# Output tiles of three query blocks: feed-forward and attention part added in one PSUM bank, with the gate ratio moved into the softmax reciprocals

## The chip, the cores and the metric

The kernel runs on one core of a Trainium2 chip. The core has five engines that run side by side and meet only at semaphores: TensorE (PE, matrix products), VectorE (DVE), ScalarE (ACT), GpSimd (POOL, used here to issue DMAs) and SyncE (SP, which issues the other DMAs). Matrix products land in PSUM, which has eight banks of 128 partitions x 512 fp32. The metric is the device time of one execution in microseconds; the number before is the median of three runs.

## The reference

One input x (2048 rows of 512 numbers) goes through two branches whose results are mixed by a gate, a number per row.

```python
g = sigmoid((x * gate_w).sum(-1, keepdims=True))
a = softmax(q @ k^T / 4) @ v, for 32 heads of 16 numbers, then @ wo      # q, k, v = x @ wqkv
b = (silu(x @ w_gate) * (x @ w_up)) @ w_down                             # 1792 columns inside
out = g * a + (1 - g) * b
```

Nearly all of the work on elements is the softmax: 32 heads x 2048 queries x 2048 keys, 134 million exponentials.

## The kernel before, in words

**Units and tiles.** The 2048 queries are cut into four blocks of 512 (`QB`, numbers 0 to 3), the heads into eight groups of four (`G`). A unit is one block with one group; there are 32 (`UNIT`). The first group of all four blocks comes first, then blocks 0, 1, 2, 3 with their other seven groups each. A unit has 16 slots, one for each 128 keys (`KT`); a slot is one tile: four heads x 128 keys x 512 queries of scores, so there are 512 tiles in all.

**Two ways to the exponential.** Most tiles go to ScalarE: `emit_pair` makes two heads' scores in one double bank `s_t` (two of them take turns), and one ACTIVATE of 128x1024 writes the exponentials `e_t`. A tile takes two of these. The rest goes to VectorE: `emit_d` makes one head's scores in a bank `d_t`, VectorE evicts it to 16-bit integers (`y_t<-d_t`, four times for a tile), and then corrects the whole 128x2048 tile: a mask (`z_t<-y_t`), an affine step (`u_t`, `kaug` or `wd_t` `<-z_t`), a square, a product, an addition, and a last step (`y_t<-y_t`). The addition is made by an accumulating DMA from GpSimd (line 795), or, in the last unit and if the end is near, on VectorE (`add_here`). Buffers named u_t, kaug and wd_t are places for the same intermediate.

**Value products.** `pv` multiplies a tile of exponentials with the values into one bank `o_ps`, which after 16 tiles holds a unit's outputs, and, in every 32nd row, the softmax denominators. `post` copies it to `osb`. `settle` sends the rows of `osb` by DMA to `onc[qb]` (the block's attention outputs) and the denominators to DRAM (`dd`). When a block has all its groups, `recip` reads the denominators back as 128x128 (`dn`), waits until its slot, takes reciprocals (`rn`), stores them (`rr`), spreads them by DMA over the partitions (`rb`) and multiplies `onc` by them (`norm`). For block 3 it does so for the first six groups; the last two are normalised separately at the end.

**Feed-forward.** For a block, 14 chunks of 128 hidden columns each need a gate and an up product (`gu`), a tanh on ScalarE (`th<-gu`), and two VectorE steps that leave the hidden activations in `mt`. Then for each 128 queries `down_pieces` accumulates 14 steps of `w_down` in a bank `dps`; VectorE evicts it to `bblk`, scaled by 1 - g (`omg`) for blocks 0 to 2, or by exp(-logit) (`ge`) for block 3. `fin_pieces` accumulates four steps of `wo` in a bank `a_ps`; `store` evicts it as g * a_ps + bblk (`gval` is g) and sends it out. For block 3 the sum of both parts is made in PSUM at the end (`last_pieces`, `tail`): `bblk` enters through a product with the identity, and the final eviction multiplies by g, since g * exp(-logit) = 1 - g.

**What sets the order.** The program is one unrolled list for each engine; `ordered` (helper lines 158, 161 and 170 of the profile) keeps each engine's instructions in the order in which they were written. A planner written in the kernel decides that order, with assumed costs: `plan.pe`, `plan.dve` and `plan.act` are the times to which each engine is booked. Score pairs for ScalarE come first; what fits between two pairs is value products, VectorE scores or a piece of a side chain. `Pacer` holds the side chains, each with a release slot, a due slot and a condition; the chain due first is taken. `later` hands VectorE an eviction, `fill_dve` picks VectorE's next work. Three banks (`ps_m`) serve `d_t` and all side chains.

`v_unit` decides how many tiles VectorE takes: it gives a tile from the end of a unit when VectorE, by the plan, would be done with it `LEAD` (16 us) before ScalarE gets to the end of that unit, or `LAST` (11 us before the change) for the last unit. So a shorter list of VectorE work becomes more VectorE tiles and fewer ScalarE exponentials by itself.

Of the kernel before, what the change touches and what calls it, by code (L numbers as in the profile page):

```python
# [9 lines left out]
ALU = mybir.AluOpType  # L10
AX = mybir.AxisListType
BF16 = mybir.dt.bfloat16
F32 = mybir.dt.float32
# [66 lines left out]
def kernel(  # L80
# [13 lines left out]
    P = 128  # L94
    x = A_x.flatten_outer_dims()
    S, D = x.shape
    F = B_w_gate.shape[1]
    DH = 16
    H = D // DH
    G = H // 4  # L100
    NB = H // 8
    DC = D // P
    FC = F // P
    KT = S // P
    QBW = 512
    QB = S // QBW
    TQ = QBW // P
    assert H * DH == D and D % P == 0 and F % P == 0 and S % QBW == 0 and G == 8 and TQ == 4
    out_f = out.flatten_outer_dims()
# [3 lines left out]
    SLOTS = UNITS * KT  # L113

    UNIT = [(qb, 0) for qb in range(QB)] + [(qb, g) for qb in range(QB) for g in range(1, G)]
# [165 lines left out]
    gval = const.tile([P, KT], F32, name="gval")  # L281
    omg = const.tile([P, KT], F32, name="omg")
    ge = const.tile([P, KT], F32, name="ge")
    bblk = big.tile([P, TQ, D], BF16, name="bblk")


# [20 lines left out]
    def later(cost, f, ready=None, key=None):  # L307

        c = plan.chain
        if c is not None:  # L310
            c.owed += 1
        ready = plan.pe + 0.25 if ready is None else ready
        owed.insert(sum(o[0] <= ready for o in owed), (ready, cost, f, c, key))
# [101 lines left out]
    def columns(n, name, lhs, rhs, end, c0=0):  # L415

        st = {}

        def pc(k):
            def f():  # L420
                if k == 0:
                    st["p"] = m_tile(name)
                w, r = lhs(k), rhs(k)
                for j in range(4):
                    mm(st["p"][32 * j:32 * j + 32, c0:QBW], lhsT=w[:, 32 * j:32 * j + 32], rhs=r, start=(k == 0),
                       stop=(k == n - 1), tile_position=(0, 32 * j), skip_group_check=True)
                spend("C", 1)
                if k == n - 1:
                    end(st["p"])
            return f  # L430
        return [(1, pc(k), k == 0) for k in range(n)]
# [180 lines left out]
    def gate_pieces(t0):  # L612
        def f():
            gp = m_tile("glog")
            for t in (t0, t0 + 1):
                for dc in range(DC):
                    mm(gp[:, t:t + 1], lhsT=xT[:, dc, t * P:(t + 1) * P],
                       rhs=gw_col[:, dc:dc + 1], start=(dc == 0), stop=(dc == DC - 1))
            spend("F", 2)

            def end():
                vec.tensor_scalar(out=ge[:, t0:t0 + 2], in0=gp[:, t0:t0 + 2], scalar1=-60.0, scalar2=60.0,
                                  op0=ALU.max, op1=ALU.min)
                m_free(gp, plan.dve)
            later(0.15, end)
        return [(0.7, f, True, "F", None)]

    def gate_end():
        act(out=ge[:, :], in_=ge[:, :], func=ACT.Exp, scale=-1.0)
        plan.act += 0.2  # L630

        def end():
            vec.tensor_scalar(out=omg[:, :], in0=ge[:, :], scalar1=1.0, scalar2=None, op0=ALU.add)
            vec.reciprocal(gval[:, :], omg[:, :])
            vec.tensor_tensor(out=omg[:, :], in0=ge[:, :], in1=gval[:, :], op=ALU.mult)
        later(0.5, end, plan.act + 0.2)


    FS = [(qb, fc) for qb in range(QB) for fc in range(FC)]
    w_gate, w_up, gs_of = {}, {}, {}  # L640

    def w_load(i, gate):
# [31 lines left out]
    scaled = set()  # L674

    def down_pieces(qb, tq):

        def end(p):
            t, n = tq, qb * TQ + tq
            share = omg if qb < QB - 1 else ge  # L680
            vec.tensor_scalar(out=bblk[:, t, :], in0=p[:, 0:D], scalar1=share[:, n:n + 1],
                              scalar2=None, op0=ALU.mult)
            if qb == QB - 1:
                scaled.add(t)
            m_free(p, plan.dve)
        return columns(FC, "dps", lambda fc: mt[:, fc, tq * P:(tq + 1) * P], lambda fc: wd_t[:, fc, :],
                       lambda p: later(0.65, lambda: end(p)))
# [238 lines left out]
    def recip16(o, i):  # L926
        with nc.allow_low_precision(reason="bf16 reciprocal of softmax denominators is plenty accurate here"):
            vec.reciprocal(o, i)

    def recip(qb, g1, n0):  # L930

        n = 4 * g1
        dn = work.tile([P, P], BF16, tag="dn", name="dn")
        queue.dma_start(out=dn[0:4 * n, :], in_=dds[qb][0:n, :].rearrange("h (a c) -> (h a) c", c=P))

        def spread():
            rn = work.tile([P, P], BF16, tag="rn", name="rn")
            recip16(rn[0:4 * n, :], dn[0:4 * n, :])
            rr = dram.tile([H, QBW], BF16, tag="rr", name="rr")
            queue.dma_start(out=rr[0:n, :].rearrange("h (a c) -> (h a) c", c=P), in_=rn[0:4 * n, :])  # L940
            for b in range(g1 // 2):
                queue.dma_start(out=rb[:, b, :],
                                  in_=rr[8 * b:8 * b + 8, :].unsqueeze(1).broadcast_to([8, DH, QBW]))
        at.setdefault(n0 + 6, []).append(lambda: later(0.87, spread))
        for b in range(g1 // 2):
            def norm(b=b):
                vec.tensor_tensor(out=onc[qb][:, b, :], in0=onc[qb][:, b, :], in1=rb[:, b, :], op=ALU.mult)
                normed.add((qb, b))
            at.setdefault(n0 + 13 + b, []).append(lambda norm=norm: later(0.345, norm))

    def recip_here(osb):
# [2 lines left out]
        mm(dps[:, :], lhsT=sbc_t[:, :], rhs=osb[:, :], start=True, stop=True)  # L954
        rd = work.tile([P, QBW], BF16, tag="rd", name="rd")
        return dps, rd

    def store(t, a_ps, base, o_t=None):
        if o_t is None:
            o_t = opool.tile([P, D], BF16, tag="ot", name="o_t")[:, :]  # L960
        vec.scalar_tensor_tensor(out=o_t, in0=a_ps[:, 0:D], scalar=gval[:, t:t + 1], in1=base,
                                 op0=ALU.mult, op1=ALU.add)
        queue.dma_start(out=out_f[t * P:(t + 1) * P, :], in_=o_t)

    here_done = []
    a_ps = []
# [6 lines left out]
    def last_pieces():  # L973

        def keep(pa, pb):
            a_ps.extend([pa, pb])
        return two_banks(NB + 1, "a_l", last_rows(0), last_rows(1), keep, stop=False)
# [16 lines left out]
            w, r = last_rows(tq)(i)  # L994
            mm(a_ps[tq][:, 0:D], lhsT=w, rhs=r, start=(i == 0), stop=False)

    def fin_pieces(qb, tq):

        def end(p):
            store(qb * TQ + tq, p, bblk[:, tq, :])  # L1000
            m_free(p, plan.dve)
        return columns(NB, "a_ps", lambda b: onc[qb][:, b, tq * P:(tq + 1) * P], lambda b: wo_t[:, b, :],
                       lambda p: later(0.67, lambda: end(p)))

    kp0 = ps_s.tile([P, 2 * QBW], F32, tag="s", name="kp0")
    qp0 = m_tile("qp0")
# [164 lines left out]
    gates = [pace.add([(0.2, gate_end, False)], 40, 106, gates)]  # L1171

    prev = []
    fin_prev = []
    ffn = set()
    f0, f1 = 72, SLOTS - 8
    per = (f1 - f0) / QB
    for qb in range(QB):
        a0 = f0 + per * qb
        gus = []  # L1180
        for i in range(FC * qb, FC * qb + FC):
            gate_pcs, up_pcs = gu_chain(i)

            def first(f=gate_pcs[0][1], i=i):
                if i == 0:
                    w_load(0, True)
                    w_load(0, False)
                    w_load(1, True)
                    w_load(1, False)
                w_load(i + 2, True)  # L1190
                w_load(i + 2, False)
                f()
            for k, pcs in enumerate(([(1, first, True)] + gate_pcs[1:], up_pcs)):
                prev = [pace.add(pcs, 58, a0 + per * (0.6 if qb < QB - 1 else 0.68) * (i + 0.5 + k / 2 - FC * qb) / FC, begun=prev)]
                gus += prev
                ffn.update(prev)
        for tq in range(TQ):
            c = pace.add(down_pieces(qb, tq), 0 if qb else 100, a0 + per * (0.6 + 0.3 * (tq + 1) / TQ if qb < QB - 1 else 0.68 + 0.32 * (tq + 1) / TQ), (gus if tq == 0 else prev) + fin_prev + gates)
            prev = [c]
            ffn.add(c)  # L1200
        last = qb == QB - 1
        fin_prev = []
        if last:

            def ripe():
                return (all((qb, b) in normed for b in range(NB - 1)) and len(scaled) == TQ and here_done)
            pace.add(last_pieces(), SLOTS - KT // 2, SLOTS, prev, cond=ripe)
            break
        for tq in range(TQ):
            rel = (UNIT.index((qb, G - 1)) + 1) * KT + 24  # L1210
            dl = max(a0 + per * (0.9 + 0.1 * (tq + 1) / TQ), rel + 7 + 3 * tq)

            def cond(qb=qb):
                return all((qb, b) in normed for b in range(NB))
            fin_prev.append(pace.add(fin_pieces(qb, tq), rel, dl, prev + fin_prev, cond=cond))


    au = at_ = half = 0
# [134 lines left out]
        emit_pv(ns[0])  # L1353

    SLACK = 0.1
    LEAD, LAST = 16.0, 11.0
    TILE_US = 1.87

    def forward():
# [183 lines left out]
```

## Time and profile before

The median is 829.81 us (829.46 to 830.11). The profiled execution spans 827.6 us.

| engine | busy, us | share | main work |
|---|---|---|---|
| ScalarE | 810.9 | 98% | 844 exponentials of 128x1024, 787.6 us |
| VectorE | 794.8 | 96% | 90 tiles of exponentials; evictions |
| TensorE | 784.2 | 95% | 8115 matmuls |
| GpSimd | 102.2 | 12% | 90 accumulating DMAs |

How to read it: a group's line gives the engine, the operation, what it writes and reads, the number of instructions, then the busy time, the mean duration of one record in ns, and the engine's idle time just before them with what ended it. Records of neighbouring instructions on one engine overlap, so the duration of a record is longer than the distance to the next one. A line of waits reads "who waited <- for whom: us in total, times, longest". A line of the timeline reads start, length, engine, operation, and in brackets the idle time before it.

### The profile page before, as it was taken

The page shows a single profiled execution, that of the slowest core. Times are in us where ns is not written, and L with a number is a line of the kernel's source. Part 1 is how long each engine was busy: PE and PEld are TensorE (multiplying, and loading weights), DVE is VectorE, ACT ScalarE, POOL GpSimd, SP SyncE. Part 2 cuts the span into 40 slices and gives each one's busy share as a digit, 9 for nine tenths or more (in the row PEclk, how much of TensorE's full clock was granted, in tenths as well). Part 3 has the DMA queues.
Part 4 walks back from the last instruction along what each step waited for, and adds up shares of the span by engine and source line. Part 5 has one row for each costly group of instructions (what it writes and reads, how often), then busy time and mean ns, then how long its engine had stood idle before and what let it go on. Part 6 is the DMA issues. An engine that isn't in the chain of part 4 may idle for free. (4 is left out here: it accounts for less than half of the span.)

```text
span 827.6 us, 20391 instructions
## 1 busy us (share of the span) xinstructions
PE 784.2 (95%) x8115; PEld 232.7 (28%) x8116; DVE 794.8 (96%) x1175; ACT 810.9 (98%) x913; POOL 102.2 (12%) x124
## 2 busy tenths in 40 slices
PE   8999999999999999999999999999998999999996
PEld 3322332322222222222222222222222222222222
DVE  6899999999999999999999999999999999999994
ACT  6999999999999999999999999999999999999996
POOL 5010111100011101101110100101111101111100
PEclk9999999999999999999999999999999999999999
DMA  7034346675544445654435474544434455453333
GB/s 178 13 76 90 59 86 124 129 154 103 105 90 84 98 85 117 118 119 84 88 68 100 81 157 85 119 91 87 79 74 100 92 113 109 103 101 73 74 63 77
DMA packets 100615, 79.54 MB, mean 96 GB/s; under 512 B 75664, under 2 KB 88552, under 8 KB 100520
## 3 DMA queue, kind: packets, MB, share of 16 engines
q0 software_dynamic: 12960, 47.19, 30.8%
q1 hardware_dynamic: 85704, 30.60, 15.8%
q8 instruction: 63, 1.03, 0.5%
q10 hardware_dynamic: 1856, 0.46, 0.3%
q14 instruction: 32, 0.26, 0.1%
HBM read 21.36 MB, written 2.34 MB: 29 GB/s over the span
## 5 line engine op out<-in xcount | busy, mean ns | idle before, releaser
L161 ACT ACTIVATE e_t<-s_t 128x1024 bf16<-128x1024 f32 x844 | 787.6, 1112 | 2.3 <-PE s_t L158 2.1
L158 PE MATMUL s_t<-qx,kaug 64*128 64x512 bf16 x1336 | 273.8, 383 | 24.5 <-ACT e_t L161 21.1
L170 DVE TENSOR_SCALAR y_t<-d_t 128x512 uint16<-128x512 f32 x360 | 234.1, 679 | 1.5 <-PE d_t L158 1.2
L158 PEld LDWEIGHTS <-kaug 64*128 64x128 bf16 x2048 | 111.6, 93 | 339.0 <-issue 329.4
L158 PE MATMUL o_ps<-e_t,vaug 128*32 128x512 bf16 x1688 | 168.1, 390 | 0.3 <-DVE osb L170 0.3
L158 PE MATMUL d_t<-qx,kaug 64*128 64x512 bf16 x296 | 102.0, 380 | 2.2 <-DVE y_t L170 1.4
L795 POOL DMA_DIRECT2D y_t<-u_t x45 | 44.4, 987 | 362.1 <-PE s_t L158 169.8
L158 PEld LDWEIGHTS <-vaug 128*32 128x32 bf16 (+1 forms) x2060 | 50.7, 93 | 123.0 <-issue 122.0
L158 PE MATMUL gu<-xT,wg 128*32 128x512 bf16 x896 | 76.8, 383 | 0.0
L158 PE MATMUL dps<-wd_t,mt 128*32 128x512 bf16 x896 | 76.1, 383 | 0.1
L795 POOL DMA_DIRECT2D y_t<-kaug x39 | 40.5, 1038 | 283.6 <-DVE kaug L170 108.1
L158 PE MATMUL gu<-xT,wu 128*32 128x512 bf16 x896 | 73.4, 382 | 0.1
L170 DVE TENSOR_SCALAR y_t<-y_t 128x2048 uint16<-128x2048 uint16 x90 | 61.3, 682 | 6.9 <-DMA y_t<-u_t 3.5
L170 DVE TENSOR_SCALAR z_t<-y_t 128x2048 uint16<-128x2048 uint16 x90 | 61.7, 685 | 1.0
L170 DVE TENSOR_TENSOR u_t<-u_t 128x2048 f16<-128x2048 f16 x45 | 54.9, 1220 | 0.9
L170 DVE TENSOR_TENSOR u_t<-u_t,z_t 128x2048 f16<-128x2048 f16 x45 | 54.6, 1213 | 0.1
L170 DVE TENSOR_TENSOR kaug<-kaug 128x2048 f16<-128x2048 f16 x39 | 47.6, 1221 | 0.9
L158 PE MATMUL s_t<-q,kaug 64*128 64x512 bf16 x212 | 43.5, 383 | 4.7 <-ACT e_t L161 4.2
L170 DVE TENSOR_TENSOR kaug<-kaug,z_t 128x2048 f16<-128x2048 f16 x39 | 47.4, 1214 | 0.1
L170 DVE SCALAR_TENSOR_TENSOR mt<-gs,gu 128x512 bf16<-128x512 bf16 x56 | 38.2, 681 | 2.4
L161 ACT ACTIVATE th<-gu 128x512 bf16<-128x512 f32 x56 | 38.4, 685 | 0.0
L170 DVE SCALAR_TENSOR_TENSOR gs<-th,gu 128x512 bf16<-128x512 bf16 x56 | 37.8, 675 | 0.1
(135 smaller groups left out, 554.9 us busy)
## 6 DMA issues: line engine op xcount, KB each, us to landing
y_t<-u_t POOLq DMA_DIRECT2D x45, 512.0 KB, 5.0
y_t<-kaug POOLq DMA_DIRECT2D x39, 512.0 KB, 5.1
wg<-in_B_w_gate_dram SPq DMA_DIRECT2D x56, 128.0 KB
wu<-in_B_w_up_dram SPq DMA_DIRECT2D x56, 128.0 KB
y_t<-wd_t POOLq DMA_DIRECT2D x6, 512.0 KB, 5.0
on<-osb SPq DMA_DIRECT2D x120, 16.0 KB
rb<-rr SPq DMA_DIRECT2D x15, 128.0 KB
wd_t<-in_B_w_down_dram SPq DMA_DIRECT2D x7, 256.0 KB
```

The lines of the kernel that those rows point to most:

```text
L158: return ordered(nc.tensor.matmul(*args, **kw))
L161: ordered(nc.scalar.activation(*args, **kw))
L170: return lambda *a, **kw: ordered(f(*a, **kw))
L795: nc.gpsimd.dma_start(out=ya, in_=ua, accum_op=ALU.add)
```

## The change

It does five things.

1. For blocks 0 to 2 the four attention steps and the 14 feed-forward steps of an output tile are accumulated in one bank (`out_pieces`, bank `ops`), and one eviction, scaled by 1 - g (`omg`), writes the output. `fin_pieces` and `store` go.
2. For this the attention part has to carry g / (1 - g), so that the one factor fits both. The ratio, 1 / exp(-logit), is computed once (`odds`), written to DRAM, read back by `recip` as a tile in the shape of the denominators, and multiplied into the reciprocals. The reciprocal is therefore taken with an fp32 result, and one product is added. The limits on the logit go from 60 to 40.
3. The feed-forward of block 3 comes first (`ORDER`), since that block still keeps its feed-forward part in `bblk`; blocks 0, 1, 2 follow, whose outputs now wait for the normalised attention.
4. Due slots of the chains follow from this (0.64 of a block's time for gate and up, the rest for the outputs).
5. `LAST` goes from 11.0 to 8.5 us: the last unit gives VectorE a tile later.

It is for taking one of two evictions of twelve output tiles off VectorE.

```diff
@@ gate_pieces, gate_end
-                vec.tensor_scalar(out=ge[:, t0:t0 + 2], in0=gp[:, t0:t0 + 2], scalar1=-60.0, scalar2=60.0,
+                vec.tensor_scalar(out=ge[:, t0:t0 + 2], in0=gp[:, t0:t0 + 2], scalar1=-40.0, scalar2=40.0,
...
+            vec.reciprocal(odds[:, :], ge[:, :])
+            odds_rows.append(dram.tile([KT, P], F32, tag="odds", name="odds_d"))
+            queue.dma_start(out=odds_rows[0][:, :].rearrange("t p -> p t"), in_=odds[:, :])
...
+    ORDER = [QB - 1] + list(range(QB - 1))
+    FS = [(qb, fc) for qb in ORDER for fc in range(FC)]
@@ down_pieces
-            share = omg if qb < QB - 1 else ge
-            vec.tensor_scalar(out=bblk[:, t, :], in0=p[:, 0:D], scalar1=share[:, n:n + 1],
+            vec.tensor_scalar(out=bblk[:, t, :], in0=p[:, 0:D], scalar1=ge[:, n:n + 1],
                               scalar2=None, op0=ALU.mult)
@@ recip
         queue.dma_start(out=dn[0:4 * n, :], in_=dds[qb][0:n, :].rearrange("h (a c) -> (h a) c", c=P))
+        full = qb < QB - 1
+        if full:
+            rd = work.tile([P, QBW], BF16, tag="rd", name="rd")[:, :].bitcast(F32)
+            queue.dma_start(out=rd[:, 0:P], in_=odds_rows[0][TQ * qb:TQ * (qb + 1), :].unsqueeze(0).broadcast_to([H, TQ, P]))
...
-            recip16(rn[0:4 * n, :], dn[0:4 * n, :])
+            if full:
+                vec.reciprocal(rd[:, P:2 * P], dn[:, :])
+                vec.tensor_tensor(out=rn[:, :], in0=rd[:, P:2 * P], in1=rd[:, 0:P], op=ALU.mult)
+            else:
+                recip16(rn[0:4 * n, :], dn[0:4 * n, :])
...
-        at.setdefault(n0 + 6, []).append(lambda: later(0.87, spread))
+        at.setdefault(n0 + 6, []).append(lambda: later(1.1 if full else 0.87, spread))
@@ fin_pieces -> out_pieces
-            store(qb * TQ + tq, p, bblk[:, tq, :])
+            t = qb * TQ + tq
+            o_t = opool.tile([P, D], BF16, tag="ot", name="o_t")
+            vec.tensor_scalar(out=o_t[:, :], in0=p[:, 0:D], scalar1=omg[:, t:t + 1], scalar2=None, op0=ALU.mult)
             m_free(p, plan.dve)
-        return columns(NB, "a_ps", lambda b: onc[qb][:, b, tq * P:(tq + 1) * P], lambda b: wo_t[:, b, :],
-                       lambda p: later(0.67, lambda: end(p)))
+            queue.dma_start(out=out_f[t * P:(t + 1) * P, :], in_=o_t[:, :])
+        cs = slice(tq * P, (tq + 1) * P)
+        return columns(NB + FC, "ops", lambda k: onc[qb][:, k, cs] if k < NB else mt[:, k - NB, cs],
+                       lambda k: wo_t[:, k, :] if k < NB else wd_t[:, k - NB, :], lambda p: later(0.65, lambda: end(p)))
@@ the chains
-    for qb in range(QB):
-        a0 = f0 + per * qb
+    for pos, qb in enumerate(ORDER):
+        a0 = f0 + per * pos
...
+            def cond(qb=qb):
+                return qb == QB - 1 or all((qb, b) in normed for b in range(NB))
+            rel = 100 if pos == 0 else (UNIT.index((qb, G - 1)) + 1) * KT + 16
+            c = pace.add((out_pieces if pos else down_pieces)(qb, tq), rel, a0 + per * (0.64 + 0.36 * (tq + 1) / TQ),
+                         (gus if tq == 0 else prev) + gates, cond=cond)
@@
-    LEAD, LAST = 16.0, 11.0
+    LEAD, LAST = 16.0, 8.5
```

More of the change, by code (lines that the diff above doesn't have):

```diff
@@ L283 @@
     ge = const.tile([P, KT], F32, name="ge")
+    odds = const.tile([P, KT], F32, name="odds")
+    odds_rows = []
     bblk = big.tile([P, TQ, D], BF16, name="bblk")
@@ L635, in end @@
             vec.tensor_tensor(out=omg[:, :], in0=ge[:, :], in1=gval[:, :], op=ALU.mult)
+            vec.reciprocal(odds[:, :], ge[:, :])
+            odds_rows.append(dram.tile([KT, P], F32, tag="odds", name="odds_d"))
+            queue.dma_start(out=odds_rows[0][:, :].rearrange("t p -> p t"), in_=odds[:, :])
         later(0.5, end, plan.act + 0.2)
-    FS = [(qb, fc) for qb in range(QB) for fc in range(FC)]
+    ORDER = [QB - 1] + list(range(QB - 1))
+    FS = [(qb, fc) for qb in ORDER for fc in range(FC)]
     w_gate, w_up, gs_of = {}, {}, {}
@@ L679, in end @@
             t, n = tq, qb * TQ + tq
-            share = omg if qb < QB - 1 else ge
-            vec.tensor_scalar(out=bblk[:, t, :], in0=p[:, 0:D], scalar1=share[:, n:n + 1],
+            vec.tensor_scalar(out=bblk[:, t, :], in0=p[:, 0:D], scalar1=ge[:, n:n + 1],
                               scalar2=None, op0=ALU.mult)
-            if qb == QB - 1:
-                scaled.add(t)
+            scaled.add(t)
             m_free(p, plan.dve)
@@ L956, in recip_here @@
         return dps, rd
[L958 to L963, printed above, removed]
     here_done = []
@@ L995, in tail, with out_pieces @@
             mm(a_ps[tq][:, 0:D], lhsT=w, rhs=r, start=(i == 0), stop=False)
-    def fin_pieces(qb, tq):
+    def out_pieces(qb, tq):
         def end(p):
-            store(qb * TQ + tq, p, bblk[:, tq, :])
+            t = qb * TQ + tq
+            o_t = opool.tile([P, D], BF16, tag="ot", name="o_t")
+            vec.tensor_scalar(out=o_t[:, :], in0=p[:, 0:D], scalar1=omg[:, t:t + 1], scalar2=None, op0=ALU.mult)
             m_free(p, plan.dve)
-        return columns(NB, "a_ps", lambda b: onc[qb][:, b, tq * P:(tq + 1) * P], lambda b: wo_t[:, b, :],
-                       lambda p: later(0.67, lambda: end(p)))
+            queue.dma_start(out=out_f[t * P:(t + 1) * P, :], in_=o_t[:, :])
+        cs = slice(tq * P, (tq + 1) * P)
+        return columns(NB + FC, "ops", lambda k: onc[qb][:, k, cs] if k < NB else mt[:, k - NB, cs],
+                       lambda k: wo_t[:, k, :] if k < NB else wd_t[:, k - NB, :], lambda p: later(0.65, lambda: end(p)))
     kp0 = ps_s.tile([P, 2 * QBW], F32, tag="s", name="kp0")
@@ L1173 @@
     prev = []
-    fin_prev = []
     ffn = set()
@@ L1177 @@
     per = (f1 - f0) / QB
-    for qb in range(QB):
-        a0 = f0 + per * qb
+    for pos, qb in enumerate(ORDER):
+        a0 = f0 + per * pos
         gus = []
-        for i in range(FC * qb, FC * qb + FC):
+        for i in range(FC * pos, FC * pos + FC):
             gate_pcs, up_pcs = gu_chain(i)
@@ L1193 @@
             for k, pcs in enumerate(([(1, first, True)] + gate_pcs[1:], up_pcs)):
-                prev = [pace.add(pcs, 58, a0 + per * (0.6 if qb < QB - 1 else 0.68) * (i + 0.5 + k / 2 - FC * qb) / FC, begun=prev)]
+                prev = [pace.add(pcs, 58, a0 + per * 0.64 * (i + 0.5 + k / 2 - FC * pos) / FC, begun=prev)]
                 gus += prev
@@ L1197, with ripe @@
         for tq in range(TQ):
-            c = pace.add(down_pieces(qb, tq), 0 if qb else 100, a0 + per * (0.6 + 0.3 * (tq + 1) / TQ if qb < QB - 1 else 0.68 + 0.32 * (tq + 1) / TQ), (gus if tq == 0 else prev) + fin_prev + gates)
+            def cond(qb=qb):
[3 more added lines that the diff above has]
+                         (gus if tq == 0 else prev) + gates, cond=cond)
             prev = [c]
             ffn.add(c)
[L1201 to L1215, printed above, removed]
+            if pos == 0:
+                downs = prev
+    def ripe():
+        return (all((QB - 1, b) in normed for b in range(NB - 1)) and len(scaled) == TQ and here_done)
+    pace.add(last_pieces(), SLOTS - KT // 2, SLOTS, downs, cond=ripe)
     au = at_ = half = 0
```

## The prediction

> **What bounds the kernel now.** I read the busy shares first, then the groups of instructions, then who waited for whom on ScalarE and TensorE, and last the timelines of a quiet stretch and of the end.
>
> ```profile
> PE 784.2 (95%) x8115; PEld 232.7 (28%) x8116; DVE 794.8 (96%) x1175; ACT 810.9 (98%) x913; POOL 102.2 (12%) x124
> ...
> L161 ACT ACTIVATE e_t<-s_t 128x1024 bf16<-128x1024 f32 x844 | 787.6, 1112 | 2.3 <-PE s_t L158 2.1
> ...
> L170 DVE TENSOR_SCALAR y_t<-d_t 128x512 uint16<-128x512 f32 x360 | 234.1, 679 | 1.5 <-PE d_t L158 1.2
> ```
>
> ScalarE is busy 810.9 of 827.6 us. From the first exponential to the last it loses only 2.3 us in gaps that the profile sees. The 844 exponentials of 128x1024 are its work; another 360 quarter tiles (90 whole ones) have their exponential made on VectorE, which is at 96% as well. The two engines share one job, 512 tiles (844 / 2 + 90), so the end moves when a tile moves from one to the other.
>
> ```profile
> ACT e_t L161 <- PE s_t L158: 2.1, 5, 1.0
> ```
> ```profile
> PE s_t L158 <- ACT e_t L161: 26.3, 86, 0.8
> ...
> PE o_ps L158 <- DVE y_t L170: 1.0, 1, 1.0
> ```
>
> TensorE waits for ScalarE 86 times, ScalarE for TensorE five times: TensorE at 95% is not the bound. The second TensorE wait is the one place where VectorE's late tile reached ScalarE: the exponentials around 640 us stand 2.12 us apart instead of 0.90, so it cost 1.2 us.
>
> What an exponential costs in time is its distance from the next, since records overlap:
>
> ```profile
> 399.38 58.22 ACT L161 ACTIVATE e_t<-s_t 128x1024 bf16<-128x1024 f32 x63 [0.18 <-PE s_t L158]
> 457.39 0.70 ACT L161 ACTIVATE th<-gu 128x512 bf16<-128x512 f32 x1
> ```
>
> 63 of them take 457.39 - 399.38 = 58.0 us, 0.921 us each. Over all 785 neighbouring pairs of records the mean distance is 0.923 and the median 0.904.
>
> **What the Trainium skill says.** "ScalarE: Activation LUTs", section What ACT_TABLE_LOAD costs, gives 186 ns + 0.833 ns an element and 93 ns of overlap: 946 ns for 1024, where the trace has 1112 ns for a record and 904 to 923 between starts; I use the trace's 0.923. "VectorE: DVE Perf Modes", section The TRN2 errata, prices an operation from PSUM at 120 + 512 cycles, 658 ns; the trace agrees for the distance (234.1 / 360 = 650 ns). The same section has (N + 151) / 0.96 ns for an fp32 product of two tensors, 291 ns at 128; no row of before is that form. "DMA: Bandwidth & Descriptors", section Anatomy of one DMA, has about 2.0 us fixed for a transfer; the store of the reciprocals agrees (the queue waited 8.2 us for four, 2.05 each).
>
> **The change, part by part.**
>
> *Evictions.* For blocks 0 to 2 the kernel evicts every output tile twice:
>
> ```profile
> L170 DVE SCALAR_TENSOR_TENSOR o_t<-a_ps,gval,bblk 128x512 bf16<-128x512 f32 x12 | 8.9, 743 | 0.0
> L170 DVE TENSOR_SCALAR bblk<-dps,omg 128x512 bf16<-128x512 f32 x12 | 8.9, 741 | 0.1
> ...
> L170 DVE RECIPROCAL rn<-dn 128x128 bf16<-128x128 bf16 x3 | 2.8, 940 | 0.0
> ```
>
> The changed kernel sums 4 attention and 14 feed-forward steps in one bank and evicts once, with the form of the second row. 12 scalar_tensor_tensors go: -8.9 us on VectorE. TensorE's steps stay the same (192 + 672 matmuls, one accumulation for two), so its time stays; 12 openings of a bank fewer are a small help that I count at nothing, since TensorE is the engine that waits.
>
> *Gate ratio.* One reciprocal of 128x16 (nearest row: 0.25 us, gval) and three fp32 products of 128x128. Bounds of a product: 225 ns (the bf16 product osb<-osb,rd) and 291 ns (the skill's formula); I take the upper. The reciprocals with fp32 output I take at the 940 ns of the row above. Sum 0.25 + 3 x 0.29 = 1.1 us more.
>
> *Freed:* 8.9 - 1.1 = 7.8 us of VectorE.
>
> *What takes its place.* One tile on VectorE is four evictions (4 x 0.650), one mask (61.7 / 90 = 0.686), one affine step ((32.1 + 27.4 + 4.1) / 90 = 0.707), a square (1.220), a product (1.214) and the last step (0.681): 7.1 us. With its final addition on VectorE too, instead of by DMA, 1.22 more: 8.3 us. So 7.8 us freed hold about one tile, and the missing 0.5 us is hidden by what VectorE idles at the end (3.5 and 1.6 us before its last two steps, below). The instruction lists as built say the same: 842 exponentials for 844, 364 quarter tiles for 360, one addition on VectorE, and again 90 additions by DMA. On ScalarE, which sets the end, this is 2 x 0.923 = 1.85 us less. That is the whole gain.
>
> *The end.* Before:
>
> ```profile
> 794.69 24.10 ACT L161 ACTIVATE e_t<-s_t 128x1024 bf16<-128x1024 f32 x26
> ```
> ```profile
> 812.95 0.69 DVE L170 TENSOR_SCALAR y_t<-y_t 128x2048 uint16<-128x2048 uint16 x1 [1.55 <-DMA y_t<-kaug]
> 817.15 0.69 DVE L170 TENSOR_SCALAR y_t<-y_t 128x2048 uint16<-128x2048 uint16 x1 [3.51 <-DMA y_t<-u_t]
> ```
>
> The last VectorE tile is ready at 817.84, 0.95 us before the last exponential ends (818.79); 8.8 us of fixed tail follow. The later release (8.5 us for 11.0) puts a tile where VectorE idled. Worked out from the built order, counted from the matmul dl (797.33 before; 22 exponential pairs follow and take 21.46 us): after it 20 follow, so ScalarE ends at dl + 19.6. VectorE: reciprocals from dl + 0.9 (798.23) take 4.5, then square 1.1, four quarter evictions and a last step 3.1, product 1.1, output eviction 0.7, mask and affine 1.3, square, product and addition 3.4: 16.1. There it waits for the other tile's addition by DMA, issued at 10.7 and 5.7 later (as in the two rows above): 16.4, and two last steps: 17.7. That is about 2 us ahead of ScalarE, so the tail keeps its 8.8 us. It is also a chain without DMA in its last tile.
>
> *New wait.* Each ratio tile comes by a DMA issued right behind dn:
>
> ```profile
> 298.54 0.53 SPq L170 DMA_DIRECT2D dn<-dd  x1
> ```
> ```profile
> 303.54 0.94 DVE L170 RECIPROCAL rn<-dn 128x128 bf16<-128x128 bf16 x1
> ```
>
> dn is issued 5.0 us before VectorE gets to it. The ratio's DMA, 0.5 us behind it, lands (2.0 us) about 2 us in time. If it came late, VectorE's next quarter evictions would queue behind the waiting reciprocal, and TensorE would wait for their banks. Bounds: 0 and 3 x 1.5 us on VectorE; I take 0. The store of the ratio is 2048 packets of 4 bytes; the trace's 512 packets of 2 bytes (gw_col) took 8 ns each and were through in 1.5 us, so about 6 us, on SyncE's queue, beside weight loads that are asked for two chains ahead: 0.
>
> *Order.* Block 3 first needs no attention, and output chains wait for normalised blocks: in the built order the outputs of blocks 0, 1, 2 are evicted at units 15-17, 22-24 and 29-31, five units after each block's normalisation or more (unit 31 is the last). No wait there. Work between two score pairs on TensorE keeps its mix: stretches with three column groups (0.949 us between exponentials) go from 200 to 207, with five (0.980) from 15 to 10; the sum is about zero.
>
> *Sum:* 829.81 - 1.85 = 827.96.
>
> **The rivals.** *A, the stall goes too.* The wait at 640 us came from an addition that landed 8.2 us after its issue:
>
> ```profile
> DMA to landing us min/median/max: 4.5/5.0/8.2
> ```
>
> With another order it may meet nobody: 827.96 - 1.2 = 826.8. For: it is one event. Against: any new order of 91 tiles on a full VectorE may meet one. *B, the gain is eaten.* One or two new stalls of that size, or more small delays (15 us of the span are distances over 0.904, so 5% more of them are 0.8): 827.96 + 1.5 = 829.5, within 0.2% of before. For: VectorE has no more slack than before; its end is planned tighter. *C, slower.* The three ratio tiles arrive late and each stalls as at 640 us, and the last tile falls 1 us behind ScalarE: 827.96 + 3 x 1.2 + 1.0 = 832.6. Against: the 2 us in hand at both places.
>
> **How the numbers follow.** Forecast 0.54, A 0.15, B 0.23, C 0.08. Faster by over 0.2% is below 828.15. The forecast lies just under that, so I count 0.44 of its 0.54 there, with all of A: 0.59. The rest of it and B: 0.33 for no change. C: 0.08. The range runs from A less 0.5 to B plus 0.4: 826.3 to 829.9; C and a little of the edges stay out.
>
> **What would show it.** Right: 842 exponentials at 0.92 us, VectorE's busy time within 1 us of 794.8, the last y_t step 1 to 2 us before the last exponential ends, 8.8 us from there to the end. Wrong: a wait of o_ps for y_t over 0.5 us, a wait of rd for the ratio's DMA, a last exponential followed by idle TensorE until y_t, or a mean distance above 0.925. What I trust least is that the small delays stay as they are; 2.3 us of gaps over 844 exponentials were few.

## The result, and the profile after

The changed kernel takes 834.81 us (833.06 to 837.65), the kernel before beside it 829.65: ratio 1.0065, 95% interval 1.0035 to 1.0094. The forecast was 827.96, its range 826.3 to 829.9; the kernel became slower, not faster. Times are medians, here of four executions; one execution of 2171.78 us, in the run with a later landing below, is left out of that run's ratio.

The busy shares and the exponentials, from the page of the changed kernel:

```profile
PE 787.8 (95%) x8123; PEld 232.3 (28%) x8124; DVE 796.4 (96%) x1177; ACT 810.6 (97%) x911; POOL 104.8 (13%) x124
...
L161 ACT ACTIVATE e_t<-s_t 128x1024 bf16<-128x1024 f32 x842 | 787.2, 1108 | 6.8 <-PE s_t L158 3.4
```

The two exponentials are gone, as forecast, and the busy times stay close to those before (VectorE 1.6 us more). What is new is the idle time before the exponentials: 6.8 us for 2.3. Counted from the starts of the records, what the distances have over 0.904 us sums to 21.2 us, for 15.0 before. So 1.8 us were won and 6.2 lost on ScalarE; the tail behind the last exponential is 9.24 us for 8.76. ScalarE's waits name no single engine for the largest gap:

```profile
ACT e_t L161 <- PE s_t L158: 3.4, 8, 0.8
...
ACT e_t L161 <- remote: 2.3, 1, 2.3
```

"remote" stands where no record of the core explains the release. It lies at 196 to 199 us. Timelines of that stretch, for SyncE, VectorE, ScalarE and TensorE:

```profile
187.04 0.37 SPq L170 DMA_DIRECT2D odds_d<-odds  x1
187.47 0.93 SPq L170 DMA_DIRECT2D wd_t<-in_B_w_down_dram  x1
188.75 12.98 SPq L170 DMA_DIRECT2D kaug<-on  x8
```
```profile
198.59 0.69 DVE L170 CAST osb<-o_ps 128x512 bf16<-128x512 f32 x1 [2.40 <-remote]
```
```profile
198.69 1.02 ACT L161 ACTIVATE e_t<-s_t 128x1024 bf16<-128x1024 f32 x1 [2.33 <-remote]
```
```profile
199.33 0.40 PE L158 MATMUL o_ps<-e_t,vaug 128*32 128x512 bf16 x4 [2.33 <-DVE osb L170]
...
202.10 0.62 PE L158 MATMUL o_ps<-e_t,vaug 128*32 128x512 bf16 x4
```

The store of the gate ratio (odds_d) goes out at 187.0. The eight transfers two places behind it take SyncE 13 us to issue (kaug<-on; 4.9 us in the kernel before), in part because one of them shares the store's semaphore and waits for the store to land. First the kernel before, then SyncE's wait in the changed one:

```profile
188.72 4.93 SPq L170 DMA_DIRECT2D kaug<-on  x8
```
```profile
SPq L170 <- DMA odds_d<-odds: 2.8, 1, 2.8
```

By that semaphore the store has landed at 199.46, 12.4 us after its issue. At 196.2 VectorE, TensorE and ScalarE stop together for 2.3 to 2.4 us, and afterwards a matmul row takes 0.62 us where it took 0.40. The stages show why. The first number behind a stretch is its length, the second TensorE's busy time; the column before the last two is the granted clock:

```profile
196.00:199.00 3.00, 1.00 (x12) 0.31 (x11) 0.60 (x2) 0.67 (x2) 0.86 (x1) 1.00 0.65 74
199.00:201.10 2.10, 1.70 (x19) 0.60 (x18) 2.10 (x5) 2.10 (x4) 0.00 (x0) 1.00 1.06 210
201.10:204.50 3.40, 3.40 (x25) 0.48 (x17) 3.35 (x5) 2.67 (x4) 0.00 (x0) 0.50 0.85 162
204.50:210.00 5.50, 5.50 (x62) 1.41 (x58) 4.54 (x8) 5.20 (x7) 0.46 (x1) 1.00 0.59 140
```

TensorE idles 2.3 us and 1.8 us later its clock is halved for 3.4 us, in which it can't feed ScalarE (2.67 us busy of 3.40). From 195 to 205 us ScalarE loses 3.8 us. The Trainium skill, "TensorE: Matmul & The Clock Gate", section What's actually happening, describes such a clock gate with windows of 3.4 us, and half the clock after an idle window. The 3.4 us agree, but no window here was idle: in the one just before the halving TensorE was busy for 1.68 of 3.41 us.

```profile
197.67:201.08 3.41, 1.68 (x19) 0.60 (x18) 2.49 (x5) 2.39 (x4) 0.00 (x0) 1.00 0.90 169
```

The end, which the forecast had worked out, timeline of ScalarE and of VectorE:

```profile
784.49 38.72 ACT L161 ACTIVATE e_t<-s_t 128x1024 bf16<-128x1024 f32 x42
```
```profile
818.84 1.23 DVE L170 TENSOR_TENSOR y_t<-y_t,kaug 128x2048 uint16<-128x2048 uint16 x1
819.98 1.29 DVE L170 TENSOR_SCALAR y_t<-y_t 128x2048 uint16<-128x2048 uint16 x2
```

VectorE is done at 821.27, the last exponential at 823.21: 1.9 us ahead, about 2 forecast.

### The profile page after: what moved, and what is told of

It reads as the page before. It is cut to its first block, busy times and chain, and to the rows that moved or that the text cites. A ratio compares the mean times of both kernels' runs of the same rounds, so it can differ in the third digit from the quotient of the medians.

```text
span 832.4 us, 20393 instructions
## 1 busy us (share of the span) xinstructions
PE 787.8 (95%) x8123; PEld 232.3 (28%) x8124; DVE 796.4 (96%) x1177; ACT 810.6 (97%) x911; POOL 104.8 (13%) x124
## 5 line engine op out<-in xcount | busy, mean ns | idle before, releaser
L158 PE MATMUL s_t<-qx,kaug 64*128 64x512 bf16 x1344 | 277.4, 383 | 23.4 <-ACT e_t L161 20.4
L170 DVE TENSOR_SCALAR y_t<-d_t 128x512 uint16<-128x512 f32 x364 | 236.6, 680 | 2.3 <-PE d_t L158 2.0
L158 PE MATMUL d_t<-qx,kaug 64*128 64x512 bf16 x288 | 98.6, 380 | 2.3 <-DVE mt L170 0.7
L799 POOL DMA_DIRECT2D y_t<-u_t x45 | 48.2, 1071 | 357.9 <-PE s_t L158 201.9
L158 PE MATMUL ops<-wd_t,mt 128*32 128x512 bf16 x672 | 56.4, 383 | 0.0
L158 PE MATMUL s_t<-q,kaug 64*128 64x512 bf16 x200 | 40.2, 384 | 3.7 <-ACT e_t L161 2.8
```

The lines of the kernel that those rows point to most:

```text
L158: return ordered(nc.tensor.matmul(*args, **kw))
L170: return lambda *a, **kw: ordered(f(*a, **kw))
L799: nc.gpsimd.dma_start(out=ya, in_=ua, accum_op=ALU.add)
```

## Experiments

**First question: is it the store, or the new order of the work?** The theory from these timelines was the store; the rival, that the new order and the tighter end bring the stalls. Four kernels.

*The store alone, in the kernel before.*

```diff
             vec.tensor_tensor(out=omg[:, :], in0=ge[:, :], in1=gval[:, :], op=ALU.mult)
+            vec.reciprocal(odds[:, :], ge[:, :])
+            odds_rows.append(dram.tile([KT, P], F32, tag="odds", name="odds_d"))
+            queue.dma_start(out=odds_rows[0][:, :].rearrange("t p -> p t"), in_=odds[:, :])
```

> The kernel before plus one reciprocal of 128x16 and the changed kernel's store of it to DRAM in 2048 packets of 4 bytes; nothing reads the result, all else is as before. Store theory (the small packets hold up the DMA engines for some 12 us, engines then stall and TensorE's clock is halved for 3 us): 832 to 835 us, a clock record of 0.5 in the middle of the run, transfers issued behind the store landing up to 10 us late. Rival (the loss is in the new order of the work and the tighter end): 829.6 to 830.0, no record of a lower clock.

Measured: 835.64 us against 829.76, ratio 1.0072 (1.0058 to 1.0086). One store that nobody reads costs 5.9 us. Its timelines show the way to ScalarE more plainly than the changed kernel's do; VectorE, then TensorE, then the stage:

```profile
197.61 0.69 DVE L170 TENSOR_SCALAR y_t<-y_t 128x2048 uint16<-128x2048 uint16 x1 [4.26 <-DMA y_t<-u_t]
```
```profile
198.36 0.62 PE L158 MATMUL o_ps<-y_t,vaug 128*32 128x512 bf16 x4 [3.56 <-DVE y_t L170]
```
```profile
196.00:203.00 7.00, 4.64 (x28) 0.84 (x27) 4.22 (x6) 2.40 (x3) 0.86 (x1) 0.52 0.33 75
```
```profile
DMA to landing us min/median/max: 4.5/5.0/15.6
```

An accumulating DMA issued at 182.0, two microseconds behind the store, lands 15.6 us later instead of 5. VectorE waits for it, TensorE for VectorE, and the clock goes to 0.52; ScalarE works 2.4 of 7 us. By its semaphore the store itself landed 11.6 us after its issue.

*The same packets, 512 bytes apart.*

```diff
-            odds_rows.append(dram.tile([KT, P], F32, tag="odds", name="odds_d"))
-            queue.dma_start(out=odds_rows[0][:, :].rearrange("t p -> p t"), in_=odds[:, :])
+            odds_rows.append(dram.tile([KT, P, 128], F32, tag="odds", name="odds_d"))
+            queue.dma_start(out=odds_rows[0][:, :, 0].rearrange("t p -> p t"), in_=odds[:, :])
```

> As the run with the store alone, but each 4-byte packet goes to a 512-byte piece of DRAM of its own (same count of packets, same bytes). If the cost lies in the number of packets of 4 bytes: the same 832 to 835. If it lies in many engines writing into the same small piece of DRAM: 829.6 to 830.2, as before.

Measured: 829.22, ratio 0.9990 (0.9982 to 0.9999). No cost. The store landed 4.7 us after its issue, the eight transfers behind it are issued in their usual time, and the longest landing is the usual one:

```profile
188.43 4.96 SPq L170 DMA_DIRECT2D kaug<-on  x8
```
```profile
DMA to landing us min/median/max: 4.5/5.0/7.7
```

What all transfers moved in the 9 us from 182 us on is the last number of these lines, in GB/s; the store alone first, then with its packets 512 bytes apart:

```profile
182.00:191.00 9.00, 8.31 (x85) 2.20 (x83) 8.16 (x12) 8.42 (x10) 0.84 (x1) 1.00 0.31 28
```
```profile
182.00:191.00 9.00, 8.81 (x90) 2.46 (x88) 8.16 (x11) 9.00 (x11) 0.71 (x1) 1.00 0.68 137
```

So it isn't the count of packets, nor their size, but how close together they land in DRAM. Why that costs is not shown: the pitch also spreads the whole store, from 8 KB over 1 MB, and no run tells neighbours that share a small piece from 2048 writes into one small area.

*The changed kernel with the ratio stored as it lies* (weights of other rows reach the outputs).

```diff
-            queue.dma_start(out=odds_rows[0][:, :].rearrange("t p -> p t"), in_=odds[:, :])
+            queue.dma_start(out=odds_rows[0][:, :].rearrange("t p -> (t p)").rearrange("(p t) -> p t", t=KT), in_=odds[:, :])
```

> The changed kernel with one line altered: the gate ratio is stored as it lies, 128 packets of 64 bytes, so that DRAM holds it in the wrong order and the attention part of the outputs is weighted with other rows' ratios; every instruction, wait and transfer is otherwise the same. Store theory: the loss of 4 to 5 us goes, 829.0 to 830.5, no lower clock in the middle of the run; with the forecast's gain untouched it would be 828.0. Rival (new order, tighter end): stays at 834 to 836.

Measured: 829.80, ratio 1.0004 (0.9995 to 1.0013). The store landed 1.4 us after its issue, and no lower clock stands in the middle of the run. With every engine's list unchanged, one store is worth 834.81 - 829.80 = 5.0 us; the interval of the changed kernel's ratio, from four executions, leaves about 2.5 us of doubt either way. But the time stops at that of before: the 1.85 us are missing.

*The ratio turned on TensorE and stored in rows.*

```diff
-            queue.dma_start(out=odds_rows[0][:, :].rearrange("t p -> p t"), in_=odds[:, :])
...
+            def turn_odds():
+                vec.tensor_copy(out=odds16[:, :], in_=odds[:, :])
+                op = m_tile("op")
+                mm(op[0:KT, 0:P], lhsT=odds16[:, :], rhs=ident[:, :], start=True, stop=True)
...
+                    vec.tensor_copy(out=oddsr[0:KT, :], in_=op[0:KT, 0:P])
+                    m_free(op, plan.dve)
+                    queue.dma_start(out=odds_rows[0][:, :], in_=oddsr[0:KT, :])
...
```

> The changed kernel with the gate ratio turned on TensorE (one matmul against the identity, one eviction of 16x128) and stored as 16 rows of 512 bytes. It adds 0.3 us of VectorE work, and the planner then makes the last tile's addition by DMA again instead of on VectorE. Store theory: 828.5 to 830.5. Rival: 834 to 836.

Measured: 841.64, ratio 1.0140 (1.0122 to 1.0159). Neither theory forecast this. Its waits of TensorE:

```profile
PE gu L158 <- DMA wg<-in_B_w_gate_dram: 6.4, 2, 4.6
...
PE op L158 <- DVE odds L170: 2.4, 1, 2.4
```

0.3 us more of VectorE work gave another order from there on. In it, TensorE waits 2.4 us for the ratio itself (the planner had not booked the copy ahead of that matmul), and later twice for feed-forward weights that SyncE issued behind other transfers; the clock was halved after each of the three. The planner has no account of SyncE's queue.

**Second question: where are the 1.85 us?** Four kernels.

*The complete change with a harmless store,* lists of all engines but SyncE as in the changed kernel.

```diff
-            queue.dma_start(out=odds_rows[0][:, :].rearrange("t p -> p t"), in_=odds[:, :])
+            odds_far.append(dram.tile([KT, P, P], F32, tag="far", name="odds_far"))
+            queue.dma_start(out=odds_far[0][:, :, 0].rearrange("t p -> p t"), in_=odds[:, :])
...
+            at.setdefault(plan.slot + 6, []).append(
+                lambda: queue.dma_start(out=oddsr, in_=odds_far[0][:, :, 0]))
+            at.setdefault(plan.slot + 12, []).append(
+                lambda: queue.dma_start(out=odds_rows[0][:, :], in_=oddsr))
```

> The changed kernel, complete, with the gate ratio stored in three transfers: 4-byte packets into pieces of 512 bytes of their own, read back as 16 rows into SBUF six slots later, stored as 16 rows of 512 bytes six slots after that. Every engine but SyncE has the same instructions in the same order. If only the 4-byte writes into shared small pieces of DRAM cost: as the flat store, 829.2 to 830.4, no lower clock in the middle. If any run of 2048 small packets in this order hurts: 832 or more.

Measured: 830.77, ratio 1.0014 (1.0008 to 1.0021). The 4-byte writes with room between them are harmless here too; the two more transfers may cost up to 1 us.

*The late release taken back* (flat store).

```diff
-    LEAD, LAST = 16.0, 8.5
+    LEAD, LAST = 16.0, 11.0
```

> The changed kernel with the flat store (ratio in the wrong order in DRAM, as before) and the release of the last unit's tile put back from 8.5 to 11.0 us. As built it has 844 exponentials on ScalarE again and 90 tiles on VectorE; all engines run the same lists up to the last 25 us. If the freed evictions are worth anything only through this release: 829.8 plus 1.85, 831.2 to 832.2. If the shorter VectorE list gains by itself: 829.8 or less.

Measured: 831.99, ratio 1.0027 (1.0019 to 1.0035): 2.2 us above the flat store, where 1.85 were forecast for two exponentials. Its page:

```profile
PE 787.5 (95%) x8128; PEld 233.5 (28%) x8128; DVE 788.3 (95%) x1167; ACT 811.7 (98%) x913; POOL 104.9 (13%) x124
```

VectorE is at 788.3 us, for 794.8 before: the evictions freed 6.5 us (7.8 forecast), and these lie idle. The description of `v_unit` above says that a shorter VectorE list becomes more VectorE tiles by itself; here it did so only through the release. (In the kernel before, 8.5 for 11.0 alone builds the same lists, so there the release gives VectorE no further tile.) So all of the change without store and release costs 831.99 - 829.61 = 2.4 us.

*The spreading of the reciprocals left out* (flat store; the attention outputs are scaled by stale numbers).

```diff
-            for b in range(g1 // 2):
-                queue.dma_start(out=rb[:, b, :],
-                                  in_=rr[8 * b:8 * b + 8, :].unsqueeze(1).broadcast_to([8, DH, QBW]))
```

> The changed kernel with the flat store and without the spreading of the reciprocals over the partitions (15 transfers of 128 KB in packets of 256 bytes are left out, so the attention outputs are multiplied by stale numbers). The engines' lists are the same. If the additions by DMA that land late beside this traffic are what eats the gain: the stall of 1.5 us at 495 us goes, 828.0 to 828.8. If the late additions have another cause: 829.8.

Measured: 828.32, ratio 0.9986 (0.9978 to 0.9994), 1.5 us under the flat store. What it removes, from the flat store's timelines of VectorE and TensorE:

```profile
495.09 0.69 DVE L170 TENSOR_SCALAR y_t<-y_t 128x2048 uint16<-128x2048 uint16 x1 [1.54 <-DMA y_t<-u_t]
```
```profile
495.84 0.40 PE L158 MATMUL o_ps<-y_t,vaug 128*32 128x512 bf16 x4 [0.48 <-DVE y_t L170]
```

That addition went out at 487.6, one microsecond behind the four transfers of 128 KB that spread the reciprocals, and landed 7.5 us later; the exponentials there stand 1.5 us too far apart. (These transfers go in packets of 1024 bytes, not of 256 as expected above: without them the trace has 1920 packets of 1024 bytes fewer and as many of 256 as before.) Without the spreading this addition is no longer late and the gap is gone. Two more gaps of the flat store's profile, 0.5 us at 672 and 1.1 us at 776 us, vanish or shrink too, so the 1.5 us of the whole run need not be this one addition's. Nor is the spreading the only traffic beside which additions are late: the one that cost the kernel before 1.2 us at 640 us went out at 630.8 beside feed-forward weights in packets of 256 bytes, 28 us ahead of that block's spreading, and in the run without spreading one addition at 132.7 us still took 8.0 us to land.

*The planner told of a later landing,* in the complete kernel with the harmless store.

```diff
-    ADD_US = 6.0
+    ADD_US = 7.5
```

> The complete changed kernel with the three-transfer store, and the planner told that an addition by DMA takes 7.5 us instead of 6.0, so that it puts the last step of each VectorE tile and the value product behind it later. Order differs from the third tile on; 842 exponentials. If late additions eat the gain: no wait of o_ps for y_t over 0.3 us, 827.5 to 828.8. If any new order of the lists brings stalls of its own: 829 to 833.

Measured: 827.86, ratio 0.9975 (0.9965 to 0.9985). Its profile has one wait of o_ps for y_t, of 0.3 us, and what the distances have over 0.904 us sums to 14.9 us, as before the change. This is the fastest version of the study.

**Third question: is that the change, or the planning?** Four kernels: the kernel before with the same edit at 7.5 and at 6.5, the complete kernel with the harmless store at 6.5, and the store once more with 64 bytes between packets (`[KT, P, 16]` in place of `[KT, P, 128]`).

> The kernel before with the planned landing of an addition at 7.5 us instead of 6.0: 844 exponentials as before, another order. If the planned landing is worth something by itself: 828.0 to 829.0, and the changed kernel's part of the 1.75 us is what is left. If the gain of the run with the change is its two exponentials: 829.3 to 830.3, so that the change is worth 1.85 us at equal planning.

> The kernel before with the planned landing at 6.5 us: 844 exponentials, a third order. Measures how far a new order alone moves the time: 829 to 832 if orders bring stalls of their own, 829.3 to 830.0 if not.

> The complete changed kernel with the three-transfer store and the planned landing at 6.5 us: 842 exponentials, a third order. At equal stalls 1.85 us below the kernel before at 6.5; if orders scatter by more than that, anywhere from 827.5 to 832.

> The kernel before plus the store in 2048 packets of 4 bytes, each into a piece of 64 bytes of its own (512 bytes in the run that cost nothing, 4 bytes in the one that cost 5.9 us). If packets hurt only when they share a piece of up to 64 bytes: 829.2 to 830.2. If larger pieces count (256 or 512 bytes): 831 to 836.

| planned landing, us | kernel before | complete change, harmless store | change of the ratio |
|---|---|---|---|
| 6.0 | 829.61, 1 | 830.77, 1.0014 (1.0008 to 1.0021) | +0.0014 |
| 6.5 | 829.50, 1.0000 (0.9992 to 1.0008) | 830.24, 1.0013 (1.0007 to 1.0019) | +0.0013 |
| 7.5 | 829.98, 1.0013 (1.0007 to 1.0020) | 827.86, 0.9975 (0.9965 to 0.9985) | -0.0038 |

The edit alone makes the kernel before slower, so the 827.86 isn't the planning's own. But at equal planning the change costs 0.1% in two orders and gains 0.4% in the third, with 842 exponentials for 844 in all three; why the third suits it is open. Over the three orders the kernel before moves by 0.1%, the changed one by 0.4%, 3.2 us. Each order has its own stalls: the profile of the kernel before at 7.5 loses 1.8 us at 352 us, after which the clock is halved for 3.4 us. Not every stall belongs to the order: the one of 1.2 us at 640 us in the kernel before is missing in the profile of the store 512 bytes apart, which differs only by that store and its reciprocal. A gain of 1.85 us is of the size of what an order brings by chance.

The store at 64 bytes' distance: 828.81, ratio 0.9994 (0.9986 to 1.0002), and it landed 4.8 us after its issue. 64 bytes are enough; pitches between 4 and 64 were not tried.

## Why the prediction was wrong

- **The step that failed is the store of the ratio**, "the trace's 512 packets of 2 bytes (gw_col) took 8 ns each and were through in 1.5 us, so about 6 us, on SyncE's queue [...]: 0". It measured +5.9 us alone and 5.0 in the change. gw_col reads DRAM; the ratio writes it. The packets' records again last 7 ns each and end within 2.5 us of the issue, so no row of the store looks slow; but it landed 11.6 us (alone) and 12.4 us (in the change) after its issue, twice the 6 us, and the cost is in what comes behind: from 190 to 200 us, packets of 1024 bytes, 46 ns as a rule, took up to 2.7 us. A price per packet from a read was carried to a write with neighbours 4 bytes apart, and the only thing asked was who waits for the store, not what runs behind it on the same DMA engines.
- **"That is the whole gain", 1.85 us**: right in mechanism and size, 842 exponentials and 2.2 us when the release alone is taken back. The forecast joined it to the freed evictions; in the run with the release taken back they bring no further tile by themselves.
- **Rival B, the gain eaten**, was given 0.23 for "new stalls of that size". It is what happens once the store is harmless: +2.4 us without the release, of which 1.5 goes with the traffic that spreads the reciprocals. The remaining 0.9 us is not traced.
- **"The sum is about zero"** for the order of TensorE's work looked at counts of columns between score pairs; it can't see when an addition meets other traffic (1.5 us in the flat store), nor SyncE's queue (two waits, 6.4 us, in the run stored in rows).
- **Rival C** had the right sign for another reason: the ratio tiles' DMA kept nobody waiting (reciprocals rd<-dn start without a wait), and the last tile was early.
- **The small prices**: the three fp32 products take 291 to 293 ns each, as taken; the page that the forecast names has the formula for an fp32 addition, not for a product. The 2.0 us of fixed time stand on their page for transfers issued by GpSimd; the ratio's go out from SyncE, so what carries that estimate is the trace's own 2.05 us. The VectorE end is 1.9 us ahead (2 forecast). VectorE's busy time moved by 1.6 us where I had said within 1: the freed evictions were 6.5 us for 7.8, the further tile 7.9 for 8.3. Of the signs of being wrong, a mean distance above 0.925 came (0.931); a wait of o_ps for y_t over 0.5 us did not.

In sum, by medians: 829.65 + 2.3 (order and its stalls, to 831.99) - 2.2 (release) + 5.0 (store) = 834.8. The terms are differences between neighbouring runs, so they add up by construction.

Open: in the changed kernel's own profile TensorE's signal for a matmul recorded at 195.4 comes at 198.56, with no late landing behind it. That the DMA traffic of the store held it there is argued from the place and from the control with the flat store, not shown. Two other runs (the store at 64 bytes, the one without spreading) show a stall near 146 us with a halved clock whose cause I did not follow.

## What to carry to other kernels

Cost a small store by what its writes do to the transfers behind it, not by its packets' own times: store whole rows or the data as it lies, or leave 64 bytes between scattered elements. When work is taken off an engine, ask which rule of the kernel turns the room into time, and try that rule alone. When an order is planned in advance and every engine is full, a gain of 0.2% has to be measured in several orders before it is believed.

## What the runs showed of the hardware

- 2048 writes of 4 bytes into DRAM, 4 bytes apart: landed 11.6 us after the issue, 5.9 us of run time; 64 or 512 bytes apart: landed after 4.8 and 4.7 us, no cost (ratios 0.9994 and 0.9990). Another transfer landed 10.6 us late (15.6 for 5.0).
- TensorE's clock was halved for 3.41 us, or twice that. Counted in steps of 3.41 us from the first clock record, what went before was a step in which TensorE was about half busy, not an idle one. All traces together have eight halvings in the middle of a run: by the records, TensorE was busy for 39 to 56% of the step before in seven of them, and for 72% in one (the store at 64 bytes). In the middle of the runs no step under 60% left a full clock behind it. So two stalls of nearly one length can end differently: 1.8 us at 352 us in the kernel before at 7.5 (first line, the clock was halved next) and 1.5 us at 495 us in the flat store (second line, it was not):

```profile
351.65:355.06 3.41, 1.82 (x22) 0.56 (x18) 3.38 (x6) 1.82 (x3) 0.86 (x1) 1.00 0.11 39
```
```profile
495.27:498.68 3.41, 2.06 (x25) 0.53 (x20) 3.41 (x8) 2.17 (x3) 0.00 (x0) 1.00 0.28 67
```

- Such a stall with the halved clock behind it cost ScalarE 1.3 to 1.6 times the stall alone: 3.8 us for 2.4 in the changed kernel, 5.1 for 4.1 with the store alone, 2.9 for 1.8 in the kernel before at 7.5.
- An accumulating DMA of 512 KB lands in 5.0 us as a rule. Late ones took 7.5 us beside packets of 1024 bytes (the spreading, flat store), 8.2 beside packets of 256 bytes (weights, the kernel before) and 8.0 beside packets of 4096 bytes (kaug<-on, the run without spreading), so no one packet size stands out.
